# Products of a constant table in TensorE's longer planned waits, in a two-layer FFT and state-space network

## The chip, the cores and the metric

The kernel runs on one core of one Trainium2 chip. The metric is the device time of one execution in microseconds (us). The engines are called as the profile calls them: PE is TensorE (PEld its weight loads), DVE is VectorE, ACT is ScalarE, POOL is GpSimd and SP is SyncE, which here only issues DMAs. PSUM, where PE writes its results, has eight banks of 512 f32 per partition.

## The reference

The input x has 2048 rows of 512 values. Four steps follow each other, each of them x = x + f(layernorm(x)): A, B, A, B.

- A is a two-dimensional real FFT over rows and columns, a product with a table of complex weights, and the inverse FFT.
- B is a long convolution along the 2048 rows, one filter for each of the 512 columns. The filter is K[d, l] = Re(sum over n of C[d, n] exp(dt[d] A[d, n] l) dt[d] B[d, n]) with 128 terms n. It is applied with an FFT of twice the length, and u * Dskip is added.

```python
def _A_ref(x, w_r, w_i):
    X = rfft2(x) * (w_r + 1j * w_i)
    return irfft2(X, s=(S, D))

def _B_ref(u, ...):
    P = exp((dt * A)[:, :, None] * l[None, None, :])
    K = einsum("dn,dnl,dn->dl", Cc, P, dt * Bc).real
    y = irfft2(rfft(u padded) * rfft(K padded))[..., :L]
    return y + u * Dskip

x = x + _A_ref(_layernorm(x), A_w_r, A_w_i)
x = x + _B_ref(_layernorm(x), ...)
x = x + _A_ref(_layernorm(x), A_w_r, A_w_i)
x = x + _B_ref(_layernorm(x), ...)
```

## The kernel before

All FFTs are matrix products with constant tables on PE, in f32. A transform of 2048 is split in two smaller ones, and the second is done in groups with their own phase tables.

**Stages, with their times in the profile.** Line numbers are those of the kernel before.

- Up to about 47 us the first layer A reads x, normalises each of its 16 parts and multiplies it with the table cRa (`forward_a`, L562, L570, L571). The same time sees the set-up of the factors of the filter K on DVE and ACT (`setup_a`, `setup_b`, `setup_f` with its casts L1022).
- From 47 to about 330 us two things are interleaved on PE: the 16 groups of layer A (`first_a`: L589, L686 to L690, L711 to L719) and the 32 units in which K is made. A unit multiplies factors on PE (L1137, bf16), takes exponentials and sines on ACT (L1153, L1167, L1172, L1173), products on DVE and POOL (L1169, L1180, L1184, L1185), and sums over n on PE (L1197). Four units form a batch. Between them K is transformed (L1265, L827).
- From there to about 376 us the inverse of layer A (`inv_a`: L743, L764) and the first transform of layer B (`forward_b`: L794) are done, from 376 to about 504 us the groups of layer B (`group_b`) and its inverse (`inv_b`).
- In `group_b` PE makes a spectrum (L827), DVE multiplies it with that of K (L926), POOL adds real and imaginary parts (L932), PE transforms back (L943), and ACT copies the result to SBUF (L952). `inv_b` loads the result back, turned by DMA, and multiplies it with cRbT (L974); DVE adds it to x (L980).
- From about 504 to 656 us the second layer A runs, and from there to the end the second layer B.

**What sets the order.** The program writes out all instructions itself; there is no scheduler behind it. Each stage is a Python generator, a "piece", that yields what its next step needs (engines, a ring of SBUF slots, a kind of PSUM bank, an event) and then emits its instructions. `Clock.run` (L385 on) takes, of the pieces that could go now, the one with the best rank. When a step could go, and when it ends, is told by a model of costs: for each engine a fixed time and a time per element (`COST`). `self.free["PE"]` is the model's time at which PE is done with all that was emitted; `t` is the time at which the step about to be emitted can start. What the model takes for a wait of PE is t minus that. PSUM banks are handed out by kind: `self.slots["p:" + kind]` lists the free ones with the model's time of their release. The model decides the order alone; on the chip each instruction waits for semaphores.

`load_ra` (L523) loads the 128x128 table cRa to `Ra[:, 1]`, right after the first part of x.

Of the kernel before, what the change touches and what calls it, by code (L numbers as in the profile page):

```python
# [41 lines left out]
RANK = -4, 0.3, 6, 1.2, 25, 0.5, 24, 0.5  # L42

NEAR = 0.1

WORK = 17664

# [148 lines left out]
class Clock:  # L196
# [165 lines left out]
    def time(self, ready, needs):  # L362
# [19 lines left out]
                    ready = max(ready, sorted(slots)[names.count(name) - 1][0])  # L382
        return ready

    def run(self, plan):  # L385

        pieces = [[rank, i, 0.0, (), piece] for i, (rank, piece) in enumerate(plan)]
        while pieces:
            ready = [(t, p) for p in pieces if (t := self.time(p[2], p[3])) is not None]
            assert ready, [p[4].__name__ for p in pieces]  # L390
            now = min(t for t, _ in ready) + NEAR
            t, p = min((e for e in ready if e[0] <= now), key=lambda e: e[1][:2])
            self.piece = p[4]
            needs = next(p[4], self)
            end = self.note(t)
            if not (isinstance(needs, str) and needs[:1] == "+"):
                p[2] = end
            if needs is self:
                pieces.remove(p)
                self.drops += [k for k, h in self.held.items() if h[2] is p[4] and k not in self.drops]  # L400
            else:
                p[3] = needs if isinstance(needs, tuple) else () if needs is None else (needs,)
            self.release()


class Net:
# [28 lines left out]
    def psum(self, kind):  # L435
        kind = self.same.get(kind, kind)

        banks = self.banks[kind]

        def make(i):  # L440
            o = 512 * banks[i]
            return self.ps[:, o:o + (1024 if kind in "aw" else 512)]
        return self.timer.tile("p:" + kind, make, len(banks))

    def drop(self, *tiles):

# [1060 lines left out]
```

## Time and profile before

| what | value |
|---|---|
| three runs | 777.12, 776.33, 777.0 us; median 777.0 |
| the profiled execution | 776.02 us, its span 774.1 us |
| instructions in the profile | 23215 |
| PE busy | 643.5 us in 9892 matmul rows |
| DVE, ACT, POOL busy | 495.2, 417.4, 305.2 us |
| TensorE clock granted, mean | 0.936 |
| DMA | 132.49 MB, mean 171 GB/s |

The span goes from the first to the last instruction of the program; the time holds some 1.9 us more around it. A row of a group or of the timeline gives the start, the busy time, the engine, the line, the operation, what it writes and reads (out<-in), the shapes and how many; in square brackets stands how long the engine was idle before it and who ended that. An f32 matmul of the program is two rows of MATMUL in the profile, a bf16 one is one. A stretch (a window of the trace) gives its length and then the busy time of PE, PEld, DVE, ACT and POOL with their rows in brackets, the clock granted to PE, the share of the DMA engines that were busy, and GB/s. The chain is the work that ended last, followed back.

### The profile page before, as it was taken

The numbers are of one execution on the slowest core, as the hardware profiler recorded it, in microseconds if no ns is written. First come the engines' busy times: TensorE is split into PE (matmuls) and PEld (weight loads), VectorE is DVE, ScalarE is ACT, GpSimd is POOL, SyncE is SP. The second block draws the span as 40 slices with busy tenths as digits, with TensorE's granted clock in tenths as the row PEclk, the third lists the DMA queues.
The fourth block names the chain that finished last, engine by engine and source line by source line (L and its number), as shares of the span: only waits on it lengthen the run. The fifth ranks groups of instructions, "written<-read, shape, count | busy, mean of one in ns | idle before, by whom it ended". The sixth has DMA issues, their size and how long they took to land. (4 is left out here: it accounts for less than half of the span.)

```text
span 774.1 us, 23215 instructions
## 1 busy us (share of the span) xinstructions
PE 643.5 (83%) x9892; PEld 416.2 (54%) x9892; DVE 495.2 (64%) x896; ACT 417.4 (54%) x759; POOL 305.2 (39%) x339
## 2 busy tenths in 40 slices
PE   3987988797986889988796886899978898878896
PEld 3875655545543444446343452778766553444565
DVE  6586778848757594985434453686776598376622
ACT  4775898878987968835242323266544333424120
POOL 3930436526435440410224423155555553066420
PEclk9998999988998899999798898999999999899999
DMA  9614411532352568637988991860655524786948
GB/s 333 214 45 138 141 48 62 178 105 86 129 178 69 203 239 286 206 106 157 236 211 269 254 273 59 210 235 1 222 209 194 175 66 101 172 211 189 250 107 278
DMA packets 76695, 132.49 MB, mean 171 GB/s; under 512 B 4684, under 2 KB 53584, under 8 KB 75952
## 3 DMA queue, kind: packets, MB, share of 16 engines
q1 hardware_dynamic: 59184, 103.74, 43.7%
q10 hardware_dynamic: 17408, 27.27, 13.3%
q8 instruction: 78, 1.28, 0.7%
q14 instruction: 25, 0.20, 0.1%
HBM read 70.31 MB, written 27.13 MB: 126 GB/s over the span
## 5 line engine op out<-in xcount | busy, mean ns | idle before, releaser
L1184 POOL TENSOR_TENSOR Y<-wk,Y 128x1024 f32<-128x1024 f32 x32 | 65.0, 2030 | 96.8 <-ACT wk L1172 36.8
L932 POOL TENSOR_TENSOR wk<-wk 128x512 f32<-128x512 f32 x32 | 39.9, 1271 | 111.0 <-DVE wk L926 98.1
L974 PE MATMUL ps<-wk,cRbT 64*128 64x256 f32 x512 | 64.4, 398 | 8.3 <-issue 3.0
L794 PE MATMUL ps<-wk,cRb 128*32 128x256 f32 x1024 | 63.0, 395 | 5.8 <-ACT wk L796 2.7
L796 ACT COPY wk<-ps 128x512 f32<-128x512 f32 x64 | 37.0, 589 | 55.8 <-PE ps L794 46.2
L926 DVE TENSOR_TENSOR wk<-ps,Y 128x1024 f32<-128x1024 f32 x32 | 37.5, 1218 | 46.2 <-PE ps L827 27.6
L974 PEld LDWEIGHTS ps<-wk,cRbT 64*128 64x128 f32 x512 | 53.2, 195 | 19.9 <-issue 11.4
L1169 DVE SCALAR_TENSOR_TENSOR wk<-wk,ps 128x1024 f32<-128x1024 f32 x32 | 38.8, 1213 | 32.1 <-ACT wk L1167 32.1
L794 PEld LDWEIGHTS ps<-wk,cRb 128*32 128x32 f32 x1024 | 36.5, 113 | 34.0 <-issue 4.9
L926 DVE TENSOR_TENSOR Y<-ps,wk 128x1024 f32<-128x1024 f32 x32 | 37.4, 1218 | 22.4 <-issue 16.5
L980 DVE TENSOR_TENSOR x<-x,ps 128x256 f32<-128x256 f32 x64 | 24.8, 407 | 41.3 <-PE ps L974 41.0
L1153 ACT ACTIVATE Y<-ps 128x1024 f32<-128x1024 f32 x48 | 46.7, 1026 | 8.2 <-PE ps L1137 8.0
L562 PE MATMUL ps<-cRa,wk 128*128 128x256 f32 x128 | 35.8, 405 | 18.3 <-POOL wk L544 13.4
L1137 PE MATMUL ps<-wk,Y 96*128 96x512 bf16 x128 | 41.7, 409 | 11.1 <-DVE Y L1180 10.1
L743 PE MATMUL ps<-cDaT,apart 128*32 128x256 f32 (+1 forms) x256 | 48.0, 336 | 1.6 <-DVE wk L1208 0.8
L1197 PEld LDWEIGHTS ps<-Y 128*32 128x32 f32 x2048 | 33.9, 119 | 25.0 <-issue 9.8
L943 PE MATMUL ps<-wk,Y 32*32 32x256 f32 x1344 | 37.8, 417 | 11.0 <-POOL wk L932 7.4
L1265 PE MATMUL ps<-wk,cRk 128*128 128x512 f32 x64 | 36.7, 700 | 11.2 <-DVE Y L1180 9.6
L932 POOL TENSOR_TENSOR wk<-Y 128x512 f32<-128x512 f32 x22 | 27.5, 1277 | 41.8 <-DVE Y L926 32.0
L1197 PE MATMUL ps<-Y 128*32 128x64 f32 x2048 | 39.1, 234 | 5.9 <-DVE x L771 2.7
L952 ACT COPY Ya<-ps 128x256 f32<-128x256 f32 x64 | 19.6, 384 | 44.5 <-PE ps L943 28.7
L700 POOL TENSOR_TENSOR x<-x 128x257 f32<-128x257 f32 x16 | 11.4, 712 | 80.4 <-PE ps L719 42.3
(216 smaller groups left out, 1650.9 us busy)
## 6 DMA issues: line engine op xcount, KB each, us to landing
Y<-in_GA_dram SPq DMA_DIRECT2D x12, 899.0 KB
x<-in_PA_dram SPq DMA_DIRECT2D x16, 642.0 KB
x<-in_A_x_dram SPq DMA_DIRECT2D x16, 512.0 KB
wk<-yk SPq DMA_DIRECT2D x16, 512.0 KB
wk<-khat SPq DMA_DIRECT2D x16, 512.0 KB
yk<-wk SPq DMA_DIRECT2D x24, 256.0 KB
kd<-wk SPq DMA_DIRECT2D x4, 1024.0 KB
khat<-wk SPq DMA_DIRECT2D x8, 512.0 KB
```

What stands on the lines that cost most here:

```text
L743: nc.tensor.matmul(p[32 * i:32 * i + 32, o:o + n], self.folded(r, i)[:, b, s2].rearrange("p g m -> p (g m)"), self.DaT[:, b, first:first + ...
L794: self.nc.tensor.matmul(p[o:o + 32, 256 * h:256 * h + 256], self.Rb[:, 2 * h + j, 32 * a:32 * a + 32], xn[s], start=True, stop=True)
L796: self.nc.scalar.copy(y[:, j, :], p)
L926: nc.vector.tensor_tensor(t[c], x, kh[:, :, ::-1, :] if c else kh, op=OP.mult)
L932: nc.gpsimd.tensor_tensor(Z[:, :, c], t[0][:, :, c], t[1][:, :, c], op=op)
L943: nc.tensor.matmul(v[j][h][i:i + 32], gi[o:o + 32, j, 4 + 2 * s + c, :], Z[o:o + 32, j, c, :], start=c == 0, stop=c == 1)
L974: nc.tensor.matmul(q[s], self.RbT[o, i, :], y[o, i, :], start=i == 0, stop=i == 3)
L1137: self.nc.tensor.matmul(p, f[:, c:c + 128], self.oh[:k, o:o + 512], start=True, stop=True)
L1153: nc.scalar.activation(m[:, :, 1024:] if i == 2 else m[:, i, :1024], p.rearrange("p (i m) -> p i m", i=2) if i == 2 else p, AF.Exp)
L1169: nc.vector.scalar_tensor_tensor(s, c, MAGIC, p, op0=OP.subtract, op1=OP.subtract)
L1184: nc.gpsimd.tensor_tensor(E[:, 0, :1024], c, m[:, :1024], op=OP.mult)
L1197: nc.tensor.matmul(pk[32 * j:32 * j + 32, 64 * e:64 * e + 64], E1[:, r, i, :], E2[:, r, i], start=r == 0, stop=r == 1)
```

## The change

`Clock.run` calls a new function, `fill`, ahead of each step that names PE among its needs. If the model has PE waiting longer than 1.0 us for that step, and some PSUM bank is free by the time PE falls idle, `fill` emits products of cRa with itself, 128x128 by 128x128 in f32, into the first 128 columns of the bank that has been free longest. Their number is the model's wait times 0.6 divided by 0.25 us; for the first group of the program, where the model's time is 0, it is 24. Nobody reads the results: whoever uses the bank next overwrites them. `self.note(start)` puts their time on the model's clock. `bank` is cut out of `psum`, so that `fill` can name a bank without taking it.

```diff
+FILL = 1.0, 0.6, 0.25
...
+    def fill(self, t):
+
+        start = self.free.get("PE", 0.0)
+        n = int((t - start) * FILL[1] / FILL[2]) if t - start > FILL[0] else 0
+        banks = [(f, i, "p:" + kind) for kind in self.net.banks for f, i in self.slots.get("p:" + kind, [(0.0, 0)])]
+        if not n or not banks or min(banks)[0] > start:
+            return
+        n = n if start else 24
+        _, i, name = min(banks)
+        p, R = self.net.bank(name[2:], i), self.net.Ra[:, 1]
+        for _ in range(n):
+            self.net.nc.tensor.matmul(p[:, :128], R, R, start=True, stop=True)
+        self.note(start)
...
             t, p = min((e for e in ready if e[0] <= now), key=lambda e: e[1][:2])
+            if "PE" in " ".join(w for w in p[3] if isinstance(w, str)).split():
+                self.fill(t)
             self.piece = p[4]
...
-        def make(i):
-            o = 512 * banks[i]
-            return self.ps[:, o:o + (1024 if kind in "aw" else 512)]
-        return self.timer.tile("p:" + kind, make, len(banks))
+        return self.timer.tile("p:" + kind, lambda i: self.bank(kind, i), len(banks))
+
+    def bank(self, kind, i):
+        o = 512 * self.banks[kind][i]
+        return self.ps[:, o:o + (1024 if kind in "aw" else 512)]
```

The built program has 51 groups of such products, 245 in all: 24 at the start, then groups of 2 to 17. The orders of DVE, ACT, POOL and SP are the same before and after; that of PE is the same but for the groups. The lines of the kernel after are 19 higher than before from L562 on (L1137 is L1156, L943 is L962), and the products have L398.

A batch of units on PE, before (Y holds the factors and products of a unit, ps is PSUM, x and Ya belong to the groups of layer A):

```order
L589 MATMUL ps<-cDa,Ya 128x128 x2
L1197 MATMUL ps<-Y 32x64 x32
L1137 LDWEIGHTS Y
L1137 MATMUL ps<-wk,Y 128x512
L1137 LDWEIGHTS Y
L1137 MATMUL ps<-wk,Y 128x512
```

and after, the same place:

```order
L608 MATMUL ps<-cDa,Ya 128x128 x2
L1216 MATMUL ps<-Y 32x64 x32
L398 MATMUL ps<-cRa 128x128 x8
L1156 LDWEIGHTS Y
L1156 MATMUL ps<-wk,Y 128x512
L1156 LDWEIGHTS Y
L1156 MATMUL ps<-wk,Y 128x512
```

Eight products stand between the sums of one unit and the factors of the next batch; nothing else moved. In the trace of before this is the place at 102.00 us.

The groups of the first layer B on PE, before (at 405 to 420 us in the trace):

```order
L943 MATMUL ps<-wk,Y 32x256 x32
L827 MATMUL ps<-Y 32x256 x48
L943 MATMUL ps<-wk,Y 32x256 x96
L827 MATMUL ps<-Y 32x256 x16
L827 MATMUL ps<-wk 32x256 x16
```

and after:

```order
L962 MATMUL ps<-wk,Y 32x256 x32
L398 MATMUL ps<-cRa 128x128 x7
L846 MATMUL ps<-Y 32x256 x16
L398 MATMUL ps<-cRa 128x128 x4
L846 MATMUL ps<-Y 32x256 x16
L398 MATMUL ps<-cRa 128x128 x3
L846 MATMUL ps<-Y 32x256 x16
L398 MATMUL ps<-cRa 128x128 x3
L962 MATMUL ps<-wk,Y 32x256 x32
L398 MATMUL ps<-cRa 128x128 x4
L962 MATMUL ps<-wk,Y 32x256 x32
L398 MATMUL ps<-cRa 128x128 x4
```

Each step of 16 or 32 matmuls now has products ahead of it; the first of the third group of them (x3) carries a wait for ACT.

The end of the last layer on PE, before:

```order
L943 MATMUL ps<-apart,Y 32x256 x32
L974 MATMUL ps<-wk,cRbT 128x256 x8
L943 MATMUL ps<-wk 32x256 x64
L943 MATMUL ps<-apart,wk 32x256 x32
L943 MATMUL ps<-wk 32x256 x32
L974 MATMUL ps<-wk,cRbT 128x256 x88
```

and after:

```order
L962 MATMUL ps<-apart,Y 32x256 x32
L993 MATMUL ps<-wk,cRbT 128x256 x8
L962 MATMUL ps<-wk 32x256 x32
L398 MATMUL ps<-cRa 128x128 x2
L962 MATMUL ps<-wk 32x256 x32
L398 MATMUL ps<-cRa 128x128 x2
L962 MATMUL ps<-apart,wk 32x256 x32
L398 MATMUL ps<-cRa 128x128 x2
L962 MATMUL ps<-wk 32x256 x32
L993 MATMUL ps<-wk,cRbT 128x256 x88
```

Three groups of two stand in the last run of L943, ahead of the last products with cRbT.

## The prediction

> **What bounds the kernel now.** I read the page first, then TensorE's waits, then its busy time and granted clock in stretches of 3.4 us, and last the rows around single waits.
>
> Busy times of the page, and the clock of the core:
> ```profile
> PE 643.5 (83%) x9892; PEld 416.2 (54%) x9892; DVE 495.2 (64%) x896; ACT 417.4 (54%) x759; POOL 305.2 (39%) x339
> core 0: 774.1 us, clock 0.936
> ```
> No other engine comes near PE's 83%, and PE did not have its full clock: a mean of 0.936, where the stretches below show either 1.00 or 0.50, means (1 - 0.936) x 2 x 774 = 99 us at half speed.
>
> TensorE's waits, by who ended them (total, times, longest):
> ```profile
> PE ps L1137 <- DVE Y L1180: 10.1, 5, 2.8
> PE ps L1265 <- DVE Y L1180: 9.6, 3, 4.9
> PE ps L686 <- ACT Y L1022: 5.2, 1, 5.2
> ```
> Each is a few us, and none is large in the whole. What they do to the clock is larger. Five stretches of 3.4 us (PE's busy time is the first figure after the length; behind POOL's stand the granted clock, the DMA share and GB/s):
> ```profile
> 98.70:102.10 3.40, 1.20 (x65) 1.16 (x66) 3.29 (x6) 3.40 (x5) 2.19 (x2) 1.00 0.19 70
> 102.10:105.50 3.40, 3.29 (x68) 1.87 (x68) 2.58 (x5) 2.88 (x3) 3.40 (x3) 0.51 0.02 5
> 248.90:252.30 3.40, 1.10 (x26) 0.44 (x29) 3.40 (x7) 3.25 (x3) 3.40 (x3) 1.00 0.08 27
> 266.00:269.40 3.40, 1.78 (x36) 0.61 (x34) 2.23 (x3) 3.40 (x6) 3.21 (x3) 1.00 0.88 264
> 358.10:361.50 3.40, 1.70 (x30) 1.16 (x22) 0.88 (x4) 1.83 (x4) 0.00 (x0) 1.00 1.04 217
> ```
> The first, in which PE worked 1.20 of 3.4 us, is followed by one at half clock, and that one is full of work (3.29 us). So are those with 1.10 and 1.78; the one with 1.70 kept its clock. I read from this that a window under about half busy costs the next one half of its speed, and that the border is not sharp. The same seen at single instructions (three of PE, one of ACT):
> ```profile
> 102.00 1.18 PE L1137 MATMUL ps<-wk,Y 96*128 96x512 bf16 x2 [2.03 <-DVE Y L1180]
> 103.18 1.93 PE L1197 MATMUL ps<-Y 128*32 128x64 f32 x64
> 120.74 1.10 PE L1197 MATMUL ps<-Y 128*32 128x64 f32 x64
> 105.92 4.86 ACT L1153 ACTIVATE Y<-ps 128x1024 f32<-128x1024 f32 x5 [0.91 <-PE ps L1137]
> ```
> Behind a wait of 2.03 us the same 64 matmuls take 1.93 us where they take 1.10 at full clock, and ACT stands 0.91 us for what comes after them.
>
> **The change, part by part.** The order of each engine stays as it was, but for 51 groups of products, 245 in all, put on PE ahead of instructions that already stood there. No DMA is issued or moved, on no queue; no copy is added; nothing waits for a product. The first product of a group takes over, from the instruction behind it, the wait for the last reader of the bank it writes, where there was one; everything on PE stands behind that wait.
>
> The price of a product. It has the shape of L570 and L571, one matmul in two rows:
> ```profile
> 14.86 0.63 PE L571 MATMUL ps<-cRa,wk 128*128 128x128 f32 x2
> 15.29 0.64 PE L570 MATMUL ps<-cRa,wk 128*128 128x128 f32 x2
> 19.54 0.39 PE L570 MATMUL ps<-cRa,wk 128*128 128x128 f32 x2
> 19.76 0.39 PE L571 MATMUL ps<-cRa,wk 128*128 128x128 f32 x2
> 99.90 0.10 PEld L1137 LDWEIGHTS <-Y 96*128 96x128 bf16 x1
> ```
> From start to start that is 0.43 us at half clock and 0.22 at full clock. 245 x 0.22 = 54 us of new PE work, most of it inside waits: the 8 products before L1137 are 1.78 us in its wait of 2.03, the 17 before L686 are 3.8 in 5.2. A weight load that ran ahead in a wait, like the one at 99.90, now comes behind the products: 0.10 us, hidden where the products end 0.25 us early, and at most 51 x 0.10 = 5 us were it nowhere hidden; I take 0, since the nearest row hides it.
>
> What a group does to its window: the 8 that stand in the wait of 2.03 before 102.00 put 1.78 us into the stretch from 98.7, which goes from 1.20 to 2.98 of 3.4. The 9 in L1137's longest wait (2.8 us, until 250.6) begin at 247.8, so that 0.9 of them falls into 248.9 to 252.3: 1.10 becomes 2.0, above the 1.78 that dropped, but not by much.
>
> The start. The table has landed when ACT copies it at 4.83:
> ```profile
> 4.83 0.30 ACT L526 COPY cRa<-cRa 128x128 f32<-128x128 f32 x1 [2.81 <-DMA cRa<-in_cRa_dram]
> 12.57 2.08 PE L562 MATMUL ps<-cRa,wk 128*128 128x256 f32 x4 [12.57 <-POOL wk L544]
> ```
> 24 products from 4.83 on, at 0.43 us for the first 3.4 to 6.8 us (one full window must pass), end between 11.8 and 13.4, about when L562 could go, which then runs warm. But PE stands 5.2 us before L686 later on, for DVE's and ACT's set-up work. So what is won before 67 us is worth 0, with 1.5 as the other bound.
>
> From 67 to 330 us seven stretches at half clock follow a wait that is now filled. The first, the longest and the sum of the seven, and two waits of ACT:
> ```profile
> 67.01:71.40 4.39, 4.39 (x15) 3.19 (x17) 2.22 (x4) 0.00 (x0) 0.88 (x1) 0.50 0.26 70
> 236.20:242.10 5.90, 5.90 (x52) 3.80 (x53) 4.42 (x6) 2.90 (x4) 5.22 (x4) 0.50 0.30 82
> sum 27.29, PE 26.50 PEld 15.47 DVE 20.68 ACT 16.18 POOL 21.26; mean PE 3.79 PEld 2.21 DVE 2.95 ACT 2.31 POOL 3.04
> 73.28 0.59 ACT L723 COPY apart<-ps 128x512 f32<-128x512 f32 x1 [6.32 <-PE ps L719]
> 242.49 0.59 ACT L723 COPY Ya<-ps 128x512 f32<-128x512 f32 x1 [3.11 <-PE ps L719]
> ```
> At full clock this work takes half: 13.2 us less for PE. In the two long stretches ACT stands longer for PE (6.32 and 3.11) than PE would save (2.2 and 2.95), so all of it, 5.1 us, passes on. The other five hold 26.50 - 4.39 - 5.90 = 16.2 us of work. They save PE 8.1; ACT comes forward by no more than it waited, 0.91 in the one shown, which makes 4.6. I take 5.6, nearer to that end, because ACT then runs five L1153 without a gap. Together 10.7. PE will wait for DVE's L1180 as long as before, since ACT and DVE move with it.
>
> After 330 us: four stretches that follow a filled wait, and the stage where the DMA engines are fullest:
> ```profile
> 334.20:337.60 3.40, 3.27 (x32) 1.58 (x36) 3.33 (x9) 0.00 (x0) 0.00 (x0) 0.51 0.02 5
> 470.80:474.20 3.40, 3.04 (x84) 1.43 (x72) 0.00 (x0) 1.20 (x4) 0.68 (x1) 0.50 0.02 5
> 484.40:487.80 3.40, 3.40 (x44) 2.15 (x46) 0.00 (x0) 1.20 (x4) 0.00 (x0) 0.51 0.02 5
> 655.10:658.50 3.40, 3.40 (x36) 1.73 (x40) 3.30 (x8) 0.59 (x1) 0.00 (x0) 0.50 0.15 28
> 376.00:464.00 88.00, 73.53 (x1600) 38.26 (x1600) 42.31 (x53) 26.91 (x65) 32.44 (x26) 0.87 0.95 249
> ```
> Half of the work again: 1.6 at 334, 3.2 for 470 and 484 together, 1.7 at 655. Of the last I keep 0.85, because the chain goes on with a DMA of 9.78 us (next rows) that may not follow. From 376 to 464 the DMA engines are 95% busy: neither gains nor costs of PE are counted there, and between 2 us lost and 3 won stay open.
>
> The costs are groups that stand where the trace has no wait, or a shorter one (two rows of PE, then three of the chain):
> ```profile
> 472.63 1.86 PE L827 MATMUL ps<-wk 64*32 64x256 f32 x32
> 479.54 0.73 PE L943 MATMUL ps<-wk,Y 32*32 32x256 f32 x32 [0.52 <-POOL wk L932]
> 662.24 9.78 DMA Ya<-wk
> 739.49 6.08 PE ps L943 x172
> 747.53 13.37 DMA wk<-Ya
> ```
> Four products before 472.63, which waited for nothing: 0.89. Four before 479.54: 0.89 - 0.52 = 0.37. In the last run of L943 (739.49, on the chain) three groups of two: 6 x 0.22 = 1.3, and the loads of 13.37 us behind it start that much later. For the smaller ones after 656 I add 0.7, half of that again, as an estimate. Sum 3.3. What hides all other groups is the wait they stand in; where another gain shortens it, a group costs up to its own length.
>
> The sum: 10.7 + 1.6 + 3.2 + 0.85 = 16.3 won, 3.3 lost, 13 us. Two lifts are thin, the one after 248.9 and the one at 334, worth 1.2 and 1.6; for half of them I take off 1.4, and 11.6 stays. The profiled execution took 776.0 us, 1.9 around its span of 774.1; that gives 764.4, and the median of the runs shown lies 1.0 above it: 765.
>
> **Weighed against the skill.** The Trainium skill, TensorE: Matmul & The Clock Gate, section "Why this matters for your kernels", says that idle gaps of more than about 3 us between bursts send the clock back to half. The trace differs: 2.03 us were enough at 102, where the window held little other work. By the page's rule only three groups of this change could lift the clock, which is what the first rival prices.
>
> **Rivals.**
> (1) Only waits that are longer than a window's greater part count, and shorter ones drop the clock for a reason that products don't mend. Then the lifts are the two long stretches, after 67 and after 236: 5.1 us, and nothing for the 4.9 before L1265, since its group ends 2.5 us before the wait does. Less 3.3 of costs, 2 are won: 775. Against it: 1.20 of 3.4 dropped and 1.70 did not, so it is the filling that decides. For it: every filled wait keeps four tenths of its idle time.
>
> (2) The clock stays up, but ACT, DVE and the DMA engines set the pace, as ACT does from 105.92 to 110.78. One of three microseconds passes on: 16.3/3 - 3.3 = 2, again 775, or no change at all. Against it are ACT's waits for PE, 6.32 and 3.11 us.
>
> (3) Slower than before, through the groups between 406 and 420 us:
> ```profile
> 406.66 2.01 PE L827 MATMUL ps<-Y 64*32 64x256 f32 x64
> 410.43 1.10 PE L827 MATMUL ps<-Y 64*32 64x256 f32 x32 [1.76 <-DVE wk L926]
> 412.46 2.92 PE L943 MATMUL ps<-wk,Y 32*32 32x256 f32 x64 [0.94 <-ACT Y L952]
> 423.64 1.96 PE L827 MATMUL ps<-wk 64*32 64x256 f32 x32 [2.50 <-DMA wk<-in_cGk_dram]
> ```
> 17 products (3.8 us) stand before 412.46, in waits of 1.76 and 0.94. Worse, the three before 410.43 must themselves wait for ACT's copy L952, the one that L943 waits for until 412.46: L827 then starts at 413.1, and L943, behind three more products, at 414.9, 2.4 us late. 13 more products, 2.9 us, meet little waiting before 420. Some 4.5 us late is the price there, and the wait of 2.50 at 423.64 takes back at most 1.8 of it. With the 3.3 elsewhere it is 7.8 at most, and it decides where the clock gives back less than that, under half of 16.3. With nothing given back: 785. Against it: L943's 2.92 us at 412.46 are at half clock, 1.4 of which the same products would win.
>
> **How the numbers follow.** My forecast has 0.62, with 758 to 772 as its own range; rival 1 has 0.11, rival 2 0.12, a part of it within 0.2%, rival 3 0.15. A measurement of this kernel can tell 0.2%, 1.6 us, from no change, so faster means under 775.4: 0.62 + 0.10 + 0.05 = 0.77; the same 0.08; slower 0.15. The range goes from 757, where PE's whole 8.1 and the 1.5 of the start pass on and 376 to 464 gives some, to 776, which takes in the two rivals of a small gain; what is left out is mostly the third.
>
> **What would show it.** Right: a mean clock of 0.96 to 0.97; full clock behind the wait at 102; PE busy at about 643 + 54 - 27 = 670 us; ACT's 0.91 us before its second L1153 gone; L1137 still waiting for L1180, with products in that time. Wrong: half clock at the same places though the products run; the clock up but the span over 770; L562's first start after 13.5 us; the last loads later against L943's previous groups by more than 1.3 us.

## The result, and the profile after

The changed kernel takes 771.1 us, the median of 20 runs (763.74 to 778.91), beside 778.04 us for the kernel before (20 runs, 775.26 to 785.01). The ratio is 0.9877, with a 95% interval from 0.9847 to 0.9907: faster by 1.2%, about 9.6 us, where the forecast said 12. The ratio rests on the runs within 1.5% of their kernel's fastest (a mean of 769.3 us for 15 of the 20 of after, of 778.8 for all 20 of before); over all runs the means differ by 7.8 us, 1.0%. In the profiled executions it is 770.48 us against 776.02, 5.5 us, so this one profile of after shows less of the gain than the runs do.

Busy times and the products' own group on the page of after (busy and mean ns of one row, then the idle time before them), and behind them its span and mean clock:

```profile
PE 675.8 (88%) x10382; PEld 460.0 (60%) x10382; DVE 494.8 (64%) x896; ACT 416.1 (54%) x759; POOL 305.0 (40%) x339
...
L398 PE MATMUL ps<-cRa 128*128 128x128 f32 x490 | 68.7, 288 | 6.4 <-DMA cRa<-in_cRa_dram 4.6
```

```profile
core 0: 768.7 us, clock 0.978
```

DVE, ACT and POOL do what they did. PE is busy 32 us longer, and its clock rose from 0.936 to 0.978: (1 - 0.978) x 2 x 768.7 = 34 us at half speed in place of 99.

TensorE's waits after, in the same form as before (total, times, longest):

```profile
PE ps L846 <- issue: 13.7, 5, 5.4
PE ps L1284 <- DVE Y L1199: 4.7, 3, 2.3
PE ps L962 <- issue: 3.9, 2, 3.7
PE ps L1156 <- DVE Y L1199: 3.8, 2, 2.6
```

L1156 and L1284 are L1137 and L1265 of before; their waits for DVE fell from 10.1 and 9.6 us to 3.8 and 4.7, because products now stand in them. The two rows marked "issue" are new in this size: the same lines before had

```profile
PE ps L827 <- issue: 4.8, 3, 3.2
PE ps L943 <- issue: 2.4, 2, 1.7
```

"Issue" means that PE waited for nothing the profile shows. All such gaps over 0.3 us add up to 10.7 us before and to 19.2 after.

The stretches after that answer to those of before (length; busy time of PE, PEld, DVE, ACT, POOL; clock, DMA share, GB/s). Times are earlier by 5 us at 100, 12 at 240, 14 at 320 and 10 at 475 and 646:

```profile
61.80:66.40 4.60, 2.98 (x21) 2.29 (x21) 3.92 (x8) 2.10 (x4) 0.88 (x1) 1.00 0.61 201
93.55:96.96 3.41, 3.08 (x80) 2.85 (x81) 3.31 (x6) 3.41 (x5) 2.06 (x1) 1.00 0.17 64
96.96:100.37 3.41, 2.85 (x70) 1.34 (x69) 3.25 (x6) 3.38 (x4) 3.41 (x4) 1.00 0.02 5
226.00:231.90 5.90, 5.85 (x94) 3.56 (x98) 4.75 (x7) 4.47 (x6) 5.16 (x4) 1.00 0.47 159
237.10:240.51 3.41, 0.70 (x4) 0.25 (x4) 3.41 (x6) 2.11 (x3) 3.04 (x3) 1.00 0.00 0
240.51:243.93 3.42, 3.36 (x68) 2.12 (x68) 2.63 (x6) 2.26 (x2) 2.20 (x2) 0.50 0.02 5
320.60:324.00 3.40, 3.33 (x100) 2.55 (x104) 3.30 (x10) 0.00 (x0) 0.38 (x1) 1.00 0.02 5
475.10:478.50 3.40, 3.40 (x32) 3.07 (x34) 1.41 (x4) 1.14 (x4) 0.00 (x0) 1.00 0.35 70
645.30:648.70 3.40, 3.40 (x68) 2.08 (x64) 3.29 (x9) 1.76 (x3) 0.00 (x0) 1.00 0.10 19
```

Every one of these stretches now has the full clock, but for the one behind L1156's longest wait (240.51). How two of the waits are filled, in rows of PE, with two of ACT behind the first:

```profile
94.89 2.05 PE L398 MATMUL ps<-cRa 128*128 128x128 f32 x16
96.99 0.38 PE L1156 MATMUL ps<-wk,Y 96*128 96x512 bf16 x1
98.97 2.95 ACT L1172 ACTIVATE Y<-ps 128x1024 f32<-128x1024 f32 x3
103.05 2.85 ACT L1172 ACTIVATE Y<-ps 128x1024 f32<-128x1024 f32 x3 [1.12 <-PE ps L1156]
235.15 2.27 PE L398 MATMUL ps<-cRa 128*128 128x128 f32 x18
239.98 0.38 PE L1156 MATMUL ps<-wk,Y 96*128 96x512 bf16 x1 [2.55 <-DVE Y L1199]
```

At 97 the eight products fill the old wait of 2.03 us to its end. At 235 nine of them run at once and end at 237.4, and the 2.55 us that are left fall into one window, which has 0.70 us of work and drops the clock.

### The profile page after: what moved, and what is told of

Same layout as the page of the kernel before. It is cut to its first block, busy times and chain, and to the rows that moved or that the text cites. A ratio compares the mean times of both kernels' runs of the same rounds, so it can differ in the third digit from the quotient of the medians.

```text
span 768.7 us, 24184 instructions
## 1 busy us (share of the span) xinstructions
PE 675.8 (88%) x10382; PEld 460.0 (60%) x10382; DVE 494.8 (64%) x896; ACT 416.1 (54%) x759; POOL 305.0 (40%) x339
## 3 DMA queue, kind: packets, MB, share of 16 engines
q10 hardware_dynamic: 17408, 27.27, 13.4%
q8 instruction: 82, 1.34, 0.7%
## 5 line engine op out<-in xcount | busy, mean ns | idle before, releaser
L398 PE MATMUL ps<-cRa 128*128 128x128 f32 x490 | 68.7, 288 | 6.4 <-DMA cRa<-in_cRa_dram 4.6
L398 PEld LDWEIGHTS ps<-cRa 128*128 128x128 f32 x490 | 60.8, 196 | 21.0 <-issue 13.9
L993 PE MATMUL ps<-wk,cRbT 64*128 64x256 f32 x512 | 61.6, 387 | 7.1 <-DMA wk<-Ya 6.2
L813 PE MATMUL ps<-wk,cRb 128*32 128x256 f32 x1024 | 59.8, 381 | 1.4 <-DVE wk L538 1.0
L813 PEld LDWEIGHTS ps<-wk,cRb 128*32 128x32 f32 x1024 | 34.9, 109 | 26.2 <-DVE wk L538 3.4
L762 PE MATMUL ps<-cDaT,apart 128*32 128x256 f32 (+1 forms) x256 | 46.0, 328 | 1.4 <-DVE wk L1227 0.9
L1216 PEld LDWEIGHTS ps<-Y 128*32 128x32 f32 x2048 | 31.2, 112 | 23.7 <-issue 14.0
L1156 PE MATMUL ps<-wk,Y 96*128 96x512 bf16 x128 | 40.2, 388 | 5.5 <-DVE Y L1199 3.8
L1216 PE MATMUL ps<-Y 128*32 128x64 f32 x2048 | 36.3, 223 | 7.7 <-POOL Y L1204 2.8
L1191 ACT ACTIVATE wk<-wk,quarter 128x1024 f32<-128x1024 f32 x32 | 36.8, 1148 | 8.7 <-DVE wk L1189 8.6
L962 PE MATMUL ps<-wk,Y 32*32 32x256 f32 x1344 | 34.8, 399 | 7.6 <-issue 3.9
## 6 DMA issues: line engine op xcount, KB each, us to landing
wk<-yk SPq DMA_DIRECT2D x16, 512.0 KB, 12.5
```

What stands on the lines that cost most here:

```text
L398: self.net.nc.tensor.matmul(p[:, :128], R, R, start=True, stop=True)
L762: nc.tensor.matmul(p[32 * i:32 * i + 32, o:o + n], self.folded(r, i)[:, b, s2].rearrange("p g m -> p (g m)"), self.DaT[:, b, first:first + ...
L813: self.nc.tensor.matmul(p[o:o + 32, 256 * h:256 * h + 256], self.Rb[:, 2 * h + j, 32 * a:32 * a + 32], xn[s], start=True, stop=True)
L962: nc.tensor.matmul(v[j][h][i:i + 32], gi[o:o + 32, j, 4 + 2 * s + c, :], Z[o:o + 32, j, c, :], start=c == 0, stop=c == 1)
L993: nc.tensor.matmul(q[s], self.RbT[o, i, :], y[o, i, :], start=i == 0, stop=i == 3)
L1156: self.nc.tensor.matmul(p, f[:, c:c + 128], self.oh[:k, o:o + 512], start=True, stop=True)
```

## Where the lead comes and goes

PE's instructions other than the products stand in the same order in all kernels here. So for each of them the start in one profile minus the start in the profile of before tells how far ahead a kernel is there. The table has that lead at some times of the kernel before; the second line of each kernel takes the "issue" gaps out of both sides. (A gap may hide a part of another wait, so the second lines are no exact account of the gaps.) How far two profiles differ with no cause in the change is seen in second_half and pad16, which have no product between 13 and 360 us: the figure there is -2.1 to +0.1 at the times read (20 to 340 us). The kernels other than after are those of the experiments below.

| us, start in the kernel before | 20 | 90 | 340 | 400 | 452 | 505 | 652 | 690 | 735 | 762 |
|---|---|---|---|---|---|---|---|---|---|---|
| after | -1.6 | -5.0 | -13.6 | -14.4 | -9.9 | -10.8 | -9.9 | -10.7 | -5.9 | -3.7 |
| less gaps | -1.6 | -5.0 | -14.2 | -15.6 | -14.8 | -15.7 | -14.8 | -15.5 | -14.5 | -12.2 |
| after_again | -1.3 | -4.7 | -12.0 | -12.2 | -9.4 | -10.0 | -10.0 | -11.3 | -4.6 | -0.1 |
| less gaps | -1.3 | -4.7 | -12.7 | -13.8 | -12.5 | -13.4 | -13.4 | -14.7 | -11.4 | -6.9 |
| first_half | -1.2 | -4.7 | -11.7 | -12.6 | -12.5 | -11.9 | -9.3 | -9.6 | -10.8 | -8.1 |
| less gaps | -1.2 | -4.7 | -11.7 | -13.7 | -17.8 | -18.5 | -15.9 | -16.3 | -18.3 | -16.1 |
| second_half | -0.4 | -1.4 | -1.0 | -2.3 | +4.2 | +3.4 | +1.9 | +0.3 | +6.3 | +7.6 |
| less gaps | -0.4 | -1.4 | -1.0 | -2.7 | -0.6 | -1.1 | -2.6 | -4.2 | -4.1 | -2.9 |
| narrow | +2.5 | +2.4 | +4.8 | +3.7 | +12.6 | +16.5 | +16.4 | +18.9 | +22.4 | +24.1 |
| long_only | -0.6 | -1.6 | -3.5 | -3.5 | -2.3 | -2.1 | +2.0 | +2.5 | +3.4 | +7.3 |
| less gaps | -0.6 | -1.6 | -3.5 | -4.1 | -7.8 | -7.5 | -3.4 | -2.9 | -2.6 | +0.5 |
| wide | -0.3 | -3.7 | -8.8 | -10.8 | -6.5 | -10.0 | -10.3 | -10.7 | -9.5 | -8.9 |
| less gaps | -0.3 | -3.7 | -8.8 | -10.1 | -9.0 | -12.5 | -12.9 | -13.2 | -11.7 | -11.1 |
| picked | -1.2 | -4.6 | -10.6 | -11.5 | -11.1 | -10.4 | -11.3 | -11.9 | -6.6 | -6.9 |
| less gaps | -1.2 | -4.6 | -10.6 | -12.3 | -15.7 | -16.5 | -17.4 | -18.0 | -16.2 | -16.5 |
| pad16 | -0.4 | -1.5 | -1.0 | -1.1 | +1.6 | -1.6 | -1.3 | +1.3 | +4.2 | +4.1 |
| less gaps | -0.4 | -1.5 | -1.0 | -1.0 | -0.3 | -3.4 | -3.2 | -0.6 | -0.9 | -1.0 |

Read along the first two lines: after is 14.4 us ahead at 400 us and ends 3.7 ahead of the same instruction; of the 10.7 us that are lost on the way, 7.3 are in gaps of "issue". The largest of each layer B:

```profile
421.84 0.62 PE L846 MATMUL ps<-Ya,Y 64*32 64x256 f32 x2
427.84 1.53 PE L846 MATMUL ps<-Ya,Y 64*32 64x256 f32 x23 [5.38 <-issue]
704.74 1.74 PE L962 MATMUL ps<-wk,Y 32*32 32x256 f32 x54 [0.35 <-ACT Ya L971]
710.14 1.09 PE L962 MATMUL ps<-wk,Y 32*32 32x256 f32 x10 [3.66 <-issue]
```

PE stops in the middle of a run of equal matmuls, 2 of 32 in the one place and 54 of 64 in the other, and waits for no operand that the profile shows. What it stops for was not in the prediction, and half of the experiments are about it.

## The experiments

Two questions: does the gain come from the clock, and from which groups (narrow, long_only, first_half, second_half); and what takes a part of it back (the other eight). In all of these kernels the instructions other than the products stand in the order of after. All of them, with the number of products, what these add to PE's program (a product is four instructions, two weight loads and two matmuls), and the sum of the "issue" gaps over 0.3 us in the profiled execution (one gap of 2.1 to 5.1 us in each sum is of another kind, as after_again shows):

| kernel | products | instructions | median us | ratio to before [95%] | profiled: us, clock | gaps us |
|---|---|---|---|---|---|---|
| before | 0 | 0 | | 1 | 776.0, 0.936 | 10.7 |
| after | 245 | 980 | 771.1 | 0.9877 [0.9847, 0.9907] | 770.5, 0.978 | 19.2 |
| first_half | 128 | 512 | 767.6 | 0.9868 [0.9824, 0.9913] | 765.9, 0.969 | 18.6 |
| second_half | 117 | 468 | 780.6 | 1.0013 [0.9979, 1.0047] | 783.2, 0.956 | 21.1 |
| narrow | 245 | 980 | 801.1 | 1.0291 [1.0247, 1.0335] | 798.3, 0.927 | 12.8 |
| long_only | 63 | 252 | 775.2 | 0.9958 [0.9926, 0.9989] | 781.3, 0.938 | 17.5 |
| after_again | 245 | 980 | 769.8 | 0.9864 [0.9819, 0.9908] | 774.0, 0.970 | 17.5 |
| wide | 135 | 540 | 766.4 | 0.9822 [0.9784, 0.9860] | 767.2, 0.979 | 12.8 |
| picked | 158 | 632 | 769.2 | 0.9877 [0.9842, 0.9912] | 768.7, 0.964 | 20.3 |
| pad16 | 16 | 64 | 783.7 | 1.0059 [1.0025, 1.0093] | 779.8, 0.940 | 15.8 |
| pw0 | 84 | 336 | 769.5 | 0.9860 [0.9812, 0.9908] | 774.0, 0.959 | 14.9 |
| pw64 | 98 | 392 | 770.3 | 0.9900 [0.9864, 0.9937] | 771.9, 0.967 | 19.9 |
| pw128 | 116 | 464 | 768.3 | 0.9851 [0.9810, 0.9891] | 764.3, 0.978 | 14.2 |
| pw192 | 130 | 520 | 766.3 | 0.9839 [0.9799, 0.9879] | 764.3, 0.975 | 13.3 |

The runs of before that stand beside them have medians of 778.0 to 779.6 us.

### narrow: the same time on PE, but little streamed

```diff
-            self.net.nc.tensor.matmul(p[:, :128], R, R, start=True, stop=True)
+            self.net.nc.tensor.matmul(p[:, :1], R, R[:, :1], start=True, stop=True)
...
```

The planner's clock is advanced by the price of the wide product, so that the same groups stand at the same places.

> The same 51 groups and 245 products at the same places, with a moving operand of 1 column in place of 128: as many instructions and weight loads, hardly any multiplying. If the gain is the clock, it is gone: mean clock 0.93 to 0.945, ratio 1.000 to 1.010, what is above 1 being the price of the groups. If the gain has another source (the waits taken over, another start of the program), the ratio stays near 0.988.

Measured: 1.0291, slower by 23 us, with a clock of 0.927 in the profile and 0.912 to 0.920 in the other five runs. The gain is gone with the clock, as expected of that cause, but both figures miss their ranges: 1.000 to 1.010 and 0.93 to 0.945 had been named. By the table narrow is only 2.4 to 4.8 us behind the kernel before at 90 to 340 us; 12.8 us are lost from 400 to 505 and 7.7 from 652 to 762, where many groups stand in no wait or a shorter one. The place behind the wait of 2.03 us, first PE, then the two stretches that answer to 93.55 and 96.96 of after:

```profile
102.34 1.95 PE L398 MATMUL ps<-cRa 128*128 128x1 f32 x16
```

```profile
101.28:104.69 3.41, 3.23 (x81) 2.94 (x82) 3.31 (x6) 3.41 (x4) 2.35 (x2) 1.00 0.18 67
104.69:108.10 3.41, 3.19 (x68) 1.98 (x67) 2.60 (x6) 2.73 (x3) 3.41 (x3) 0.50 0.02 5
```

One-column products take nearly the same time as those of 128 columns (1.95 us for 16 rows, 2.05 after); the 128x128 weight loads in front of them take 1.86 us of it. PE counts as busy for 3.23 of 3.41 us, more than in after, and the clock still falls. So the busy time of the profile isn't what keeps the clock: 128 moving columns do where one does not. What in them is counted (columns, products, results) isn't shown. The whole traces say the same, cut into steps of 3.41 us: in before, the 22 steps at full clock with half clock behind them are busy for 1.94 us or less, and the 169 that keep it for 1.55 or more; in narrow some that are followed by half clock are busy for the whole 3.41. And with equal instructions at equal places, the difference between narrow and after, 4% of the time, is what a clock that is kept up is worth against one that such products let fall, the start included: there the 24 narrow products never raised the clock and ended at 15.0 us, so that L562 began 2.5 us late, and that stayed.

The Trainium skill, TensorE: Matmul & The Clock Gate, section "What's actually happening", puts the clock down to how busy PE has been. The traces agree for full-width products, and the row above (3.23 of 3.41 us busy, then 0.50) differs if busy is read as the profile's busy time.

### long_only: the groups of 24, 17, 11 and 11 alone

```diff
+        if start and n < 11:
+            return
```

> Only the groups of 24, 17, 11 and 11, the four that stand in waits of over 3 us (before 12.6, 67, 155.6 and 236 us). By the rival that only long waits count, this has all the clock gain of the first half and none of the later losses: ratio 0.978 to 0.985. By the theory that a filled window decides, it has the lead that after shows at these four places (1.6, 3.4, about 2 and 2.5 us) and lacks the five or six behind waits of 2 us: ratio 0.986 to 0.992.

Measured: 0.9958 [0.9926, 0.9989], 0.4% faster, a third of the whole gain. Both expectations were missed, that of the rival (0.978 to 0.985) by far and that of the filled windows (0.986 to 0.992) by less: the four leads add up to 9.5 us in after, and here the lead is 5.9 at 247 us and 3.5 at 340, in a profile that is the slowest of its twelve runs. The wait of 2.03 us is empty again, and the clock falls behind it as it did before:

```profile
98.85:102.26 3.41, 1.46 (x53) 0.81 (x56) 3.25 (x6) 3.39 (x4) 3.41 (x3) 1.00 0.02 8
102.26:105.67 3.41, 3.33 (x68) 1.70 (x61) 2.79 (x7) 2.88 (x4) 2.48 (x2) 0.50 0.03 5
```

The short groups, of 2 to 9 products in planned waits of 1 to 4 us, are worth the rest. The first rival, by which only the long waits count, falls: its interval and that of after (0.9847 to 0.9907) do not meet.

### first_half and second_half: the groups of one plan alone

```diff
-            if "PE" in " ".join(w for w in p[3] if isinstance(w, str)).split():
+            if "PE" in " ".join(w for w in p[3] if isinstance(w, str)).split() and self.net.banks is BANKS1:
```

(the 17 groups up to 361 us of the trace of before; second_half has BANKS2 there, the 34 groups behind that.)

> Only the 17 groups of the first plan are left (128 products, up to about 362 us of the trace of before); the 34 groups of layer B and the second layer A are out. In the trace of after PE leads the kernel before by 13.6 us at 340 us and by 5.4 us at the end. If the later groups themselves lose it (time where no wait is, and their instructions to be fetched), most of the 13.6 us stays: 763 to 766 us, ratio 0.980 to 0.985. If the DMA engines and fetches of layer B take it back whatever stands on PE, the end is as after's: ratio 0.985 to 0.993.

> The 34 later groups alone (117 products). By the first theory they cost what the other run keeps: 0 to 6 us slower than before, ratio 1.000 to 1.008. If they only fill waits and the loss comes from the DMA engines, they win the lifted clock windows of the second half, 2 to 4 us: ratio 0.995 to 0.998.

Measured: 0.9868 for the first, all of the gain; 1.0013 for the second, none. The second raised the clock (0.956) and is still not faster. Its lead falls by 6.5 us between 400 and 452 us, and less its gaps it is 0.4 to 4.2 us ahead at all places of the table. The two runs don't choose together between the two expectations: first_half lies, by its ratio if not by all of its interval, where the loss comes back whatever stands on PE (0.985 to 0.993), second_half where the later groups cost something (1.000 to 1.008).

### after_again: do the gaps come back?

> The kernel after once more, beside the next three. Theory F (TensorE's gaps without a releaser are waits for its own 16,384-byte instruction blocks, which come late where the DMA engines are full): the gaps between 355 and 470 us and after 695 us stand within a few us of the same instructions, since the borders of the blocks lie at the same instructions, and add up to 15 to 21 us, against 10.7 in the profile of before. Rival P (what was lost after 376 us is the length of the products that stand where nothing was waited for): the gaps come and go at random, and the lead over before still falls at the groups of 406 to 421 us and of 703 to 743 us. Ratio to before 0.985 to 0.990 by both.

The same kernel in another execution, at the places of the two gaps above:

```profile
423.12 0.62 PE L846 MATMUL ps<-Ya,Y 64*32 64x256 f32 x2
427.75 1.53 PE L846 MATMUL ps<-Ya,Y 64*32 64x256 f32 x23 [4.01 <-issue]
704.60 1.26 PE L962 MATMUL ps<-wk,Y 32*32 32x256 f32 x35
709.52 1.09 PE L962 MATMUL ps<-wk,Y 32*32 32x256 f32 x10 [3.66 <-issue]
```

Again 2 of 32, and again the last 10 of 64. Numbering PE's matmul rows in order of time, all nine gaps of the first profile stand at the same rows in the second, to the row; and in other kernels they stand at other instructions, but at like distances:

| kernel | row of each gap over 0.3 us from 380 to 465 us | from 685 us on |
|---|---|---|
| before | 5419, 5672, 5799 | 8820, 9201 |
| after | 5552, 5680, 6060 | 9211, 9337, 9592 |
| after_again | 5552, 5680, 6060 | 9211, 9337, 9592 |
| wide | 5424, 5551, 5931, 6058 | 8954, 9462 |
| pad16 | 5293, 5420, 5800 | 8948, 9202 |

The distances are 126 to 128 rows or multiples of that (5680 - 5552 = 128, 6060 - 5680 = 3 x 126.7). A matmul row has a weight load beside it, so 128 rows are 256 instructions, and a few less where the sequencer's own stand between. PE's program in after is 10382 weight loads, 10382 matmuls and 233 rows of its sequencer; the queue that carries instructions moved

```profile
q8 instruction: 82, 1.34, 0.7%
```

82 packets with 1.34 MB, or 16,384 bytes each, and 1.34 MB over 20,997 instructions is 64 bytes for one. So a block holds 256 instructions, and the gaps stand at the borders of blocks. When the blocks landed, from the packets' own records, in after:

```
gap 417.14 to 418.53   block 416.20 to 417.26, PE goes on 1.28 us behind it
gap 422.46 to 427.84   block 425.68 to 426.67, 1.18
gap 449.12 to 451.45   block 448.93 to 449.98, 1.47
gap 692.71 to 693.57   block 690.88 to 692.06, 1.51
gap 706.48 to 710.14   block 707.48 to 708.71, 1.43
```

In all 14 profiles 99 of the 113 gaps end 1.2 to 1.8 us behind such a landing. These are waits for instructions. The other 14, one in each kernel, are of another kind: the first L827 (L846 in after) of the first layer B, in before at 376.36 us. It is the same instruction in all, half a block beside the raster in before and after, carries a semaphore wait of its own, and PE goes on 0.1 to 8.2 us behind a landing. Its 3.2 us before and 3.9 after (2.1 to 5.1 in all) are in the sums of the table; what it waits for isn't shown. Without it the sums are 7.4 us before and 15.4 after.

The long waits are found where the DMA engines are full: in the 7 us ahead of each of the 36 of 1.9 us and more they were busy for 83% or more, while some of the short ones stand at 47 to 80%. The share in the 14 us around the largest of after, in tenths:

```profile
DMA  9943009999995899989899999799999899899999
```

Such a wait also costs clock. All 28 of 2.7 us or more in the 14 profiles have a stretch of half clock in them or right behind them, 3.4 or 6.8 us long. In after these are three of the nine that are left:

```profile
424.83:431.66 6.83, 3.82 (x64) 1.77 (x66) 1.60 (x2) 0.06 (x1) 0.41 (x1) 0.50 1.01 289
452.14:455.55 3.41, 3.41 (x88) 1.38 (x88) 0.00 (x0) 1.66 (x4) 0.00 (x0) 0.50 0.25 83
708.13:714.96 6.83, 4.82 (x52) 2.44 (x54) 1.68 (x2) 0.65 (x2) 1.00 (x1) 0.50 0.82 197
```

What the half clock costs there is not taken out in the lines "less gaps".

The Trainium skill, Runtime: NRT & Kernel Launch, section "Instruction fetch mechanics", states blocks of 16 KiB, 256 instructions, the next of which is fetched while the current one executes, with the cost of a border "mostly hidden". The size agrees with the 16,384 bytes and the 128 rows here; hidden it is at most of the 82 borders, and eight of them cost 15.4 us together.

### pad16: 64 instructions that cost nothing themselves

The kernel before with 16 one-column products at the start; the other groups are left out, and only the planner's clock is advanced by their time, so that the order stays:

```diff
-        n = n if start else 24
+        n = n if start else 16
...
+        self.net.groups = getattr(self.net, "groups", 0) + 1
+        if self.net.groups > 1:
+            self.take("PE", start, 0.22632 * n + 0.1 * (self.form != (128, 128)))
+            self.form = 128, 128
+            return
...
-            self.net.nc.tensor.matmul(p[:, :128], R, R, start=True, stop=True)
+            self.net.nc.tensor.matmul(p[:, :1], R, R[:, :1], start=True, stop=True)
...
```

> The kernel before with 16 one-column products of cRa at the start alone, in a time in which TensorE has nothing to do (they end before 12 us): 64 instructions more, which shift the border of each later 16,384-byte block by a quarter of a block. Clock within 0.003 of before, and all else as before. F: the gaps without a releaser move to other instructions and their sum changes by 2 us or more from 10.7; the time changes by up to 4 us in either direction. Rival (the gaps belong to the instructions at which they stand, or to nothing in the program): same places, same sum, and the time within 0.2% of before.

Measured: 1.0059 [1.0025, 1.0093], slower by 4.6 us. That is a little more than the 4 us that F allowed, and not the rival's 0.2%. In the profiles the clock is 0.940 beside 0.936, the lead is 0.4 to 1.5 us in its favour at the places of the table up to 400 us, and the gaps are 15.8 us in place of 10.7. The last of them, where before has no gap:

```profile
718.64 1.46 PE L999 MATMUL ps<-wk,cRbT 64*128 64x256 f32 x10
724.40 1.01 PE L999 MATMUL ps<-wk,cRbT 64*128 64x256 f32 x3 [4.30 <-issue]
```

The 64 instructions are executed before 12 us, when PE has nothing to do. All that they are known to change later is where a border falls. In the table of leads the whole loss (+4.1 at 762 us) is in the gaps; without them it is -1.0. So the place of the borders alone moves this kernel by some half a per cent. What is thin in this is that the gaps of one execution of each kernel stand for all, and that the mean clock of all its runs is a little lower than that of before's (0.932 and 0.936), which may be the gaps' own doing, as shown above.

### wide: the same groups in fewer instructions

```diff
-        for _ in range(n):
+        R2 = self.net.Ra.rearrange("p a m -> p (a m)")[:, 128:]
+        for _ in range(n // 2):
+            self.net.nc.tensor.matmul(p[:, :256], R, R2, start=True, stop=True)
+        if n % 2:
             self.net.nc.tensor.matmul(p[:, :128], R, R, start=True, stop=True)
...
```

> The same 51 groups of the same length, made of products with 256 columns (cRa and its negative) and one of 128 where the number is odd: 135 products, 540 instructions for TensorE in place of 980, with the same streaming time. Clock as after, 0.975 to 0.98, by both. F: fewer instructions and other borders, so the gaps without a releaser lie elsewhere and add up to less, 11 to 15 us, and the time falls by 3 to 6 us against the kernel after. P: the same time as after within 2 us, with the lead lost at the same groups.

Measured: 0.9822, 766.4 us against 769.8 for after beside it, with gaps of 12.8 us instead of 17.5. The 3.4 us lie in the expected range and go the way of the gaps; the clock, 0.984 in the mean of its six runs and 0.980 in those of after, may have a part in it. This is the fastest kernel here by its ratio. But the intervals of the two overlap (0.9784 to 0.9860 and 0.9819 to 0.9908), so that wide beats after is likely and not settled.

### picked: without the groups that stand where nothing waits

Only the first plan's 17 groups and nine later ones, from 563 to 685 us:

```diff
+        if self.net.groups > 17 and self.net.groups not in (34, 35, 36, 37, 39, 42, 44, 45, 46):
+            self.take("PE", start, 0.22632 * n + 0.1 * (self.form != (128, 128)))
+            self.form = 128, 128
+            return
```

> The 17 groups of the first plan and nine of the second (before L645, L764, L794, L846 from 563 to 685 us), 158 products; the 25 groups left out are those between 373 and 484 us and those where the trace of before shows no wait. P: the lead of 12 to 13 us at 400 us is kept to the end and grows by 2 to 3 behind 655 us: 762 to 764 us, ratio 0.980 to 0.983, 4 us better than only the first plan's groups. F: the gaps without a releaser decide and are not changed in kind by what is left out, so the ratio lies at 0.985 to 0.990 as for the kernel after and for the first plan alone.

Measured: 0.9877, no better than after, as F had it; the 762 to 764 us of P are missed. P may not be wrong in all: less its gaps picked is ahead by 16.5 us at 762 where after is by 12.2, which would put the products that it leaves out at some 4 us. But the four kernels of the next part, with the same groups, are ahead by 5.8 to 14.5 there, so that isn't settled. The borders of picked fell so that its gaps are 20.3 us, the most but one of the table.

### pw0, pw64, pw128, pw192: one kernel, four places of the borders

The groups of picked, made as in wide, with 128-column products in the first 0, 2, 7 or 12 groups (the diff is that of pw0; the other three have their number in place of 0):

```diff
...
+        pairs = n // 2 if self.net.groups > 0 else 0
+        for _ in range(pairs):
+            self.net.nc.tensor.matmul(p[:, :256], R, R2, start=True, stop=True)
+        for _ in range(n - 2 * pairs):
             self.net.nc.tensor.matmul(p[:, :128], R, R, start=True, stop=True)
...
```

> The 26 groups of picked, made of 256-column products as in wide, and 128-column ones where the number is odd: 84 products, 336 instructions, the same streaming time as picked (158 products, 632 instructions). This and the next three differ only in how many of the first groups are made of 128-column products, which shifts the block borders of TensorE's instructions by quarters of a block. Theory F: the gaps without a releaser stand at the borders, so their sum differs between the four by 4 us or more, and the times differ by the same to within 3 us; less its gaps each of the four is about 16 us ahead of before in the second layer B, as picked is. Rival P: the four agree within 2 us, at 0.985 to 0.990. For this one by F, about wide's gaps (12 to 13 us) and a time of 762 to 766 us.

> As pw0, but the first two groups of 128-column products: 98 products, borders shifted by 56 instructions against pw0. F: the gaps move to other instructions, by 28 matmul rows earlier in the program, and their sum is another; if a shift by a quarter of a block costs here what the 16 narrow products cost before, 5 us more of gaps and 767 to 771 us. P: as pw0 within 2 us.

> As pw0, but the first seven groups of 128-column products: 116 products, borders shifted by 128 instructions, half a block, against pw0. F: another sum of gaps, between 8 and 18 us, and a time of 758 to 770 us that follows it. P: as pw0 within 2 us.

> As pw0, but the first twelve groups of 128-column products: 130 products, borders shifted by 184 instructions against pw0, some three quarters of a block. F: another sum of gaps, between 8 and 18 us, and a time of 758 to 770 us that follows it. P: as pw0 within 2 us.

Measured: gaps of 14.9, 19.9, 14.2 and 13.3 us, which differ by 6.6 where 4 or more were expected; medians of 769.5, 770.3, 768.3 and 766.3 us. The kernel with the most gaps is the slowest and that with the fewest the fastest, but 4 us between them is not more than their intervals allow, so the times alone don't tell F from P here. Two expectations were missed: pw0 should have been at 762 to 766, and "about 16 us ahead less its gaps" came out as 12.5 to 15.7 around 700 us in the last three and 5.8 in pw0. Pw0's profiled execution is 4.5 us longer than its median, so its lead says least. Fewer instructions in picked's groups brought no gain that shows (0.984 to 0.990 against 0.9877), and no kernel here beats wide.

## Why the prediction was right, and where it wasn't

**The clock.** Right, and the sign follows from it. The mean clock rose to 0.978 (0.969 to 0.992 over the runs; 0.96 to 0.97 had been named), PE's busy time to 675.8 (670), the stretch behind the wait at 102 runs at full clock, ACT's 0.91 us before its second L1153 is gone. Narrow shows that it is the clock and not the presence of products. Of the signs of being wrong, "the clock up but the span over 770" is not met in the profile (768.7) but in nine of the 20 runs. What was inexact is the reading of "a window under about half busy": that holds for matmuls of full width, and narrow's windows of one-column products fail it at 3.23 of 3.41 us.

**From 67 to 340 us: 10.7 + 1.6 expected.** Between 54 and 340 us the lead grows by 10.4 us in after (from -3.2), by 9.1 and 8.9 in after_again and first_half, and by 7.0 to 9.9 in the other six kernels whose groups there fill the same waits. So 7 to 10 came, and after's first profile is the best of the nine. The stretch after 67 was put at 2.2, and the lead grows by 1.8 from 54 to 90; the long one after 236 at 2.95, and it grows by 3.7 from 187 to 247. Smaller than expected is the batch at 102: 0.9 was expected, and the lead grows by 0.4 between 90 and 150, where ACT, early now, waits 1.12 us for PE two instructions later (103.05; 0.07 before). The lift behind 248.9 was called thin and failed: 0.70 us in its window. The one at 334 held. Of the 1.4 taken off for half of these two, the first was due.

**The start, 0 expected.** Too low by up to 1 us: at 20 us the ten kernels with full-width products at the start are 0.3 to 1.6 ahead, and second_half and pad16, without them, 0.4. After's lead of 1.6 doesn't vanish in PE's later wait before L686 (2.9 at 67 us); nor does narrow's late start of 2.5 us. The bound of 1.5 about holds.

**470 and 484 us, 3.2 less 1.26 expected.** The clock rose (475.10), but from 452 to 505 us the lead grows by 0.9 only, and by 0.7 without gaps in first_half, which has no products there. The two named groups, priced at 0.89 and 0.37, cost 0.65 and 0.50 at their places, and both come back at once: waits of 1.17 us for ACT and 1.63 for POOL that followed are down to 0.30 and 0.29. So up to 484 us ACT and POOL set the pace, and the clock's gain is taken up by such waits too. By 488 PE is 1.6 us further ahead, and waits of 0.53, 0.89 and 0.72 us for the DMA that writes wk take half of that back.

**655 us, 0.85 of 1.7 expected.** The lead grows by 1.7 there (-9.9 to -11.6), all of it, and by 0.0 in first_half and pad16, which have no product there. That long_only, which has none either, also gains 1.7 (its profile has no half clock there) shows that whether a stretch drops can also differ from execution to execution.

**376 to 464 us, 0 expected, "between 2 us lost and 3 won" open.** The step that failed. The lead falls by 4.5 us between 400 and 452; without the gaps it falls by 0.8. So the larger part of it is gaps. The groups that rival 3 had named have their price too: through the 30 products between 406.66 and 420.05 us the lead falls from 14.4 to 11.4, with no gap of "issue" among them, and 1.7 comes back at 423.64, where before waits 2.50 us for a DMA. The rival had 4.5, less 1.4 won by the clock at 412.46, and at most 1.8 taken back: 3.1 and 1.8 against 3.0 and 1.7. Rival 3 fails by its own condition: the clock gave back more, 10 us before these places and some of it at them.

**Behind 656 us, 1.3 + 0.7 of costs expected.** The three groups of two in L943's last run, priced at 1.3, set PE back by 0.55 to 0.58 us each, but part of it comes back within the run: from ahead of the first to behind the third the lead falls by 0.7 to 1.0. In all, the lead without gaps falls from 665 to 762 us by 4.3 in after, 8.2 in after_again, 3.4 in wide and 1.4 in second_half, which have the same groups there, while first_half without any gains 0.2. So the 2.0 was too low in three of four, the 0.7 for the small groups above all; how much is theirs, and how much the half clock behind the gaps, isn't settled.

**What wasn't in the sum: the instructions themselves.** 245 products were priced as 54 us of PE's time and as nothing else. They are also 980 instructions, and in the two layers B PE waits for blocks of instructions at borders that these shift. This term was put at nothing, without a reason. The gaps grew by 8.5 us in the profiled execution (6.8 in the second one). The sum of the parts gave 11.6; the lead without gaps at 762 us is 12.2 in the first profile, near that, and 6.9 in the second, so in the first the gaps are what keeps the gain down. That the first comes so near is in part luck, since parts of the sum missed on both sides: the start and 655 us gave more than was put down, 470 to 505 us and the end less. That the row "issue" stood in the profile of before, with 10.7 us in all, was not used.

**The rivals.** (1) falls with long_only and the full clock behind short waits. (2), one of three microseconds passing on, falls for the first 340 us, where 7 to 10 of the 12.3 pass on; behind that it holds in part, as at 470 and 484, where 0.9 us is left. (3) had its price right and not its condition.

## What to carry to other kernels

Where a profile shows half the clock behind waits of 2 us or more, independent matmuls of full width in these waits pay, if the work behind them sets the pace; count them against a window of the clock. From the place at 235 us, where the products at the start of a wait left 2.55 us empty and the clock fell, it looks better to put them at its end; that was not tried. Price an added instruction also as an instruction: where DMA is full, see whether the gaps marked "issue" come at equal distances on the busiest engine. Filler of few long instructions is likely better, by wide against after, and not settled. Before crediting or blaming a small edit for half a per cent, shift the program by some idle instructions and see how far that alone moves it.

## What the runs showed that wasn't expected

- 64 instructions executed in an idle time at the start made the kernel 0.59% slower [0.25, 0.93], by all signs through the places of 16,384-byte blocks. The largest single wait for a block was 5.88 us, in second_half. Why a block comes late at one border and not at the next isn't shown: the trace has its landing and not its request.
- A 128x1 product keeps PE as long as a 128x128 one (1.95 and 2.05 us for 16 rows), and doesn't hold the clock.
- One kernel's mean clock varies between executions, and the time with it: after_again ran from 762.0 us of span at 0.987 to 772.2 at 0.970, in six runs on one chip. Where the windows of the clock lie against the program seems to decide that, as at 237 us; this was not tried.
